# Two head groups of attention in one burst: four bursts for eight in the hidden stage of tiles 5 and 6

## The chip, the cores and the metric

The kernel runs on one core of a Trainium2 chip. Its time is device microseconds of that core, the median of several executions; before the change three executions took 805.23, 806.70 and 808.77 us. Five engines work side by side: TensorE (PE; its weight loads are shown apart as PEld), VectorE (DVE), ScalarE (ACT), GpSimd (POOL) and SyncE (SP). In this kernel POOL and SP mostly issue DMA transfers. Each engine works off its own list of instructions, whose order is fixed when the program is built.

## The reference

Attention within chunks of 64 tokens, for 8 batches of 8 heads (576 tokens, head width 64), and then a feed-forward layer with a quadratic activation over all 4608 tokens (512 wide, hidden width 2048), all in fp32:

```
scores = scale * matmul(q_c, k_c^T)            # per head and chunk: 64 x 64
attn   = exp(scores - max) / (sum + 1e-9)
x      = matmul(attn, v_c)                     # back to (4608, 512)
h      = x @ w_in                              # 2048 wide
g      = where(h >= 1, h, where(h <= -1, 0, (h + 1)^2 / 4))
out    = g @ w_out
```

## The kernel before

The 4608 tokens are nine tiles of 512. A tile's attention is four head groups (two heads each); a group's work has a number, its turn, from 0 to 35 (`turn`, L174). For tiles 3 and later, a pair of tiles shares eight turns: tiles 7 and 8 have the turns 28 to 35.

The feed-forward layer of tiles 3 to 8 is done for pairs of tiles (3 and 4, 5 and 6, 7 and 8), by a Strassen scheme with seven products where plain blocks have eight, named P1 to P7. A pair has two stages. The hidden stage (h) has 56 products of `product` (L908), each six matmuls of 128x512: eight blocks p by seven names, ordered by `alternating` (L863), in the banks ps_h0, ps_h1 for even p and ps_o0, ps_o1 for odd p. ACT and DVE read each product's bank (`whole_last`, L1008) before the next product may write it. The output stage has 56 products of `products` (L1113), by name: P1, P2, P6, P5, P7, P3, P4, eight each. Each needs its block split into a high and a low half, by an ACT cast and a DVE subtraction (`operand_of`, L1100; they run in the helpers at L743 and L747). The banks ps_o2 and ps_o3 (the pair `o_pair`) take P1, P6, P7 and P4 of the output stage of tiles 3 and 4, and nothing in a hidden stage.

Attention of the next pair is put among the products in bursts (`burst`, L1289). A burst is the values of turn n (`values_of`, L487: attention by v) and the scores of turn n + 2 (`scores_of`, L465: q by k), both in the bank pair `a_pair` (ps_a), in matmuls of 64x64. Behind it stand the softmax of the scores (`attn_softmax`, L525: a maximum on DVE, eight exponentials on ACT at L547, sum, reciprocal, multiplication and transposition on DVE, then eight DMAs into aT, four from SP's queue and four from POOL's), a copy of the values to SBUF (`keep_x`, L766), the DVE transpositions of q and k of turn m + 1 into qT and kT (`attn_turn`, L449), and loads of v, q and k. `BURSTS` (L965) holds the numbers of the products ahead of which a burst is listed: eight in the stages of tiles 3 and 4 and eight in the hidden stage of tiles 5 and 6 (every seventh product from the fourth on). Tiles 7 and 8 have none.

The order on each engine is not the order of the listing. `Plan` (L19) takes every step with an engine, a cost in us and what it reads and writes, and emits the steps in the order in which they would start by these costs; where several are ready, the one listed first goes first (`ahead` moves a step up or down in that). So a burst that is listed later can be emitted sooner, where PE would have nothing else by these costs.

Of the kernel before, what the change touches and what calls it, by code (L numbers as in the profile page):

```python
# [134 lines left out]
def kernel(  # L135
# [23 lines left out]
    NP = H // 2  # L159
# [10 lines left out]

    BATCH = (0, 1, None, 2, 3, 4, 5, 6, 7)
    ALONE = 2

    def turn(t, g):  # L174
        if t <= ALONE:
# [82 lines left out]
    def room(name, bufs, t, g):  # L258
        if t == 0 and (name, g) in first:
            return first[name, g]  # L260
        if t > 0 and name in ("e", "x"):
            return wheel[(2 * turn(t, g) + (name == "x")) % 3]
        return bufs[turn(t, g) % len(bufs)]
# [223 lines left out]
    def values_of(t, g):  # L487


        akey, aT = room("aT", aT_bufs, t, g)  # L490
        vkey, v_sb = room("v", v_bufs, t, g)
        pkeys, pair = bank_pair_of(t, g)
        halves = aT.rearrange("p (e c q) -> p c e q", e=2, q=Q)

        def emit():
            for n in range(CT // 2):
                for h in range(2):
                    at = (2 * n + h) * C
                    of = h * HALF + n * C
                    for half in range(2):  # L500
                        rows = slice(half * C, (half + 1) * C)
                        nc.tensor.matmul(  # L502
                            out=pair[h * C:(h + 1) * C, half, HALF + n * C:HALF + (n + 1) * C],
                            lhsT=v_sb[rows, of:of + C],
                            rhs=aT[rows, at:at + C] if t == 0 else halves[rows, of // C],
                            start=True, stop=True,
                        )

        return emit, (f"{akey}_0", f"{akey}_1", vkey), pkeys

    def attn_products(*some, lag=0.0):

        plan.add(
            "pe", 0.2 + 0.6 * len(some), lambda: [emit() for emit, _, _ in some],
            [k for _, reads, _ in some for k in reads],
            [k for _, _, writes in some for k in writes],
            columns=1024 * len(some), lag=lag,
        )

    def bank_pair_of(t, g):  # L520
        if t == 0 and g % 2:
            return ("ps_o2", "ps_o3"), o_pair
        return ("ps_a0", "ps_a1"), a_pair

    def attn_softmax(t, g):  # L525
# [14 lines left out]
        if sums:  # L540
            plan.add("dve", 0.08, lambda: nc.vector.tensor_scalar_mul(mx, mx, -SCALE), (), (mkey,))  # L541

            many = 2 if t > ALONE else 1

            def exps(some):
                for n in range(some * G // many, (some + 1) * G // many):
                    nc.scalar.activation(  # L547
                        out=e3[:, n, :], in_=sc[:, n // 4, n % 4, :], func=AF.Exp, bias=mx[:, n, :],
                        scale=SCALE, accum_out=sm[:, n, :],
                    )  # L550

            for some in range(many):
                plan.add("act", 2.33 / many, lambda some=some: exps(some), (*pkeys, mkey), (ekey, skey))
        else:
            plan.add("dve", 0.6, lambda: nc.vector.tensor_tensor(
                out=e4, in0=sc, in1=mx4.broadcast_to([P, 2, G // 2, C]), op=ALU.subtract
            ), (*pkeys, mkey), (ekey,))
            plan.add("act", 0.52, lambda: nc.scalar.activation(
                out=e, in_=e, func=AF.Exp, scale=SCALE
            ), (), (ekey,))  # L560
# [36 lines left out]
    def attn_split(t, g):  # L597
        if t > ALONE:
            keep_x(t, g)
            return  # L600
        pkeys, pair = bank_pair_of(t, g)
        hkey, xh = xh_bufs[g][t % 2]
        lkey, xl = xl_bufs[g][t % 2]

        def of_tokens(x):
            return x.rearrange("p (n r q) -> p r n q", r=2, q=C)

        ps = pair[:, :, HALF:].rearrange("p r (n q) -> p r n q", q=C)
        plan.add("act", 0.48, lambda: nc.scalar.copy(out=of_tokens(xh), in_=ps), pkeys, (hkey,))
        plan.add("dve", 0.6, lambda: nc.vector.tensor_tensor(  # L610
            out=of_tokens(xl), in0=ps, in1=of_tokens(xh.bitcast(F32)), op=ALU.subtract
        ), (*pkeys, hkey), (lkey,))
# [152 lines left out]

    def keep_x(t, g):  # L766
        i = g // 2
        pkeys, pair = bank_pair_of(t, g)
        name = "eo"[g % 2] + "BA"[(t - ALONE) % 2]
        key, ap = raw_of(t, i, name)  # L770
        keep(key, ap, pkeys, pair[:, :, HALF:].rearrange("p r (n q) -> p r n q", q=C))
        if t <= ALONE + 2 and name == "oB":
            combine_whole(t, i)
# [188 lines left out]
        return f"h_{f}", lambda: held["h"][:, f, :]  # L962

    LATER = -60
    BURSTS = ((10, 17, 24, 38, 45, 52, 59, 68), range(3, 53, 7))  # L965
    sums = {
        (name, p): dram.tile([P, 2, QC], F32R, name=f"sums_{name}_{p}")
        for name in OUT_ORDER for p in range(NQ)
# [320 lines left out]
    def burst(n, m):  # L1289
# [12 lines left out]
        if m is not None and m + 2 < ALL:  # L1302
            load_heads(*AT[m + 2], "qk")

    for t in range(ALONE + 1):
        for j in range(NF):
            step = (t - 1) * NF + j
            if t == 0:
                for what, g in SECOND.get(j, ()):
                    what(*divmod(NP + g, NP))  # L1310
            elif step in SPREAD:
                n, m = SPREAD[step]
                if n is None and m == 2 * NP:
                    attn_turn(*AT[m])
                burst(n, m)
                if m is not None and m + 1 <= 3 * NP + 1:
                    attn_turn(*AT[m + 1])
            ffn_in(t, j)
            prepare_next()
            m = t * NF + j - LAG  # L1320
            if m >= 0:
                ffn_out(*divmod(m, NF))
            ffn_split(t, j)
            if step in WEIGHTS:
                combine_weights(WEIGHTS.index(step), step in AGAIN)
            if step in SUMS_AT:
                combine_out(SUMS_AT.index(step), step in AGAIN)
            if t == 1:
                for name in ("P4",) if j % 2 else ("P1", "P2"):
                    keep_factor(name, j // 2, f"split_{t}_{j}")  # L1330
            if t == ALONE and j < len(HANDED):
                hand_lot("wi", j, F32 if j < 2 else F32R, *HANDED[j])
                if j == 2:
                    hand_lot("wo", 0, F32R, "ring0")
        if t:
            take_raws((first_raw, next_raw)[t - 1], t % 2)
# [11 lines left out]
        take(f"ring_{key}", key, [P, T], F32R, (key,), (f"ring_{key}",))  # L1348

    def between(t, n):  # L1350
        if turns and n in BURSTS[(t - ALONE - 1) // 2]:
            burst(*turns.pop(0))

    turns = [(n, n + 2) for n in range((ALONE + 3) * NP, ALL - 2)] + [(ALL - 2, None), (ALL - 1, None)]
    for t in range(ALONE + 1, NTILE, 2):
        if t > ALONE + 1:
            move_blocks()
        for n, (p, name) in enumerate(alternating(0, NQ)):
            between(t, n)
            if t == ALONE + 1 and name == "P1":  # L1360
# [72 lines left out]
```

## Time and profile before

| what | before |
|---|---|
| median of three executions | 806.70 us |
| the profiled execution, whole | 805.89 us |
| its span on the core | 804.1 us |
| PE busy | 795.0 us (99% of the span) |
| DVE, ACT busy | 650.2 us (81%), 537.7 us (67%) |
| granted TensorE clock, mean | 0.999 of full speed |
| hidden stage of tiles 5 and 6 | from 486.0 us to about 568 us |

The profile shows one execution. Matmuls are pipelined: a matmul's own duration overlaps with the next, so the time from one start to the next start tells what it costs. An engine's idle time stands in brackets with what ended it. The chain of waits follows the work that ended last, back from the end, so a step that isn't on it can become longer or shorter, to some extent, with no effect.

### The profile page before, as it was taken

The numbers are of one execution on the slowest core, as the hardware profiler recorded it, in microseconds if no ns is written. First come the engines' busy times: TensorE is split into PE (matmuls) and PEld (weight loads), VectorE is DVE, ScalarE is ACT, GpSimd is POOL, SyncE is SP. The second block draws the span as 40 slices with busy tenths as digits, with TensorE's granted clock in tenths as the row PEclk, the third lists the DMA queues.
The fourth block names the chain that finished last, engine by engine and source line by source line (L and its number), as shares of the span: only waits on it lengthen the run. The fifth ranks groups of instructions, "written<-read, shape, count | busy, mean of one in ns | idle before, by whom it ended". The sixth has DMA issues, their size and how long they took to land.

```text
span 804.1 us, 16928 instructions
## 1 busy us (share of the span) xinstructions
PE 795.0 (99%) x5652; PEld 652.8 (81%) x5652; DVE 650.2 (81%) x1131; ACT 537.7 (67%) x1293; POOL 345.5 (43%) x606
## 2 busy tenths in 40 slices
PE   8999999999999999999999999999999999999997
PEld 8887788888888888888888788888888888888886
DVE  5999996768799996686899996777996955589962
ACT  5799975455576775687894665887845556686450
POOL 2122223565655464554455334545343334433340
PEclk9999999999999999999999999999999999999999
DMA  9899843887998897999999899977686896666775
GB/s 223 249 302 239 221 78 127 252 261 228 293 255 225 199 283 207 302 264 250 259 246 273 217 245 256 257 230 214 184 214 197 223 243 195 194 191 195 218 200 118
DMA packets 289495, 181.51 MB, mean 226 GB/s; under 512 B 242945, under 2 KB 254721, under 8 KB 289409
## 3 DMA queue, kind: packets, MB, share of 16 engines
q0 software_dynamic: 40640, 122.72, 48.0%
q1 hardware_dynamic: 244544, 56.93, 33.7%
q10 hardware_dynamic: 4224, 0.79, 0.6%
q8 instruction: 45, 0.74, 0.4%
q14 instruction: 42, 0.34, 0.1%
HBM read 133.17 MB, written 38.80 MB: 214 GB/s over the span
## 4 chain that ended last, share of the span: by engine, by line
PE 84%; DMA 5%; DVE 4%; SPq 3%; ACT 2%; issue 2%; POOL 1%; DVEq 0%; POOLq 0%; ACTq 0%
PE ps_o L1124 17%; PE ps_o L661 15%; PE ps_h L625 15%; PE ps_h L918 13%; PE ps_o L918 13%; PE ps_h L1124 7%; PE ps_a L502 2%; SPq L382 2%; DVE new_wi L747 2%; PE ps_a L480 2%; DMA v_sb<-in_v_dram 1%; DMA k_sb<-in_k_dram 1%; DMA words<-in_moe_w_in_dram 1%; DMA q_sb<-in_q_dram 1%; DMA ring_r<-sums_P 1%
## 5 line engine op out<-in xcount | busy, mean ns | idle before, releaser
L747 DVE TENSOR_TENSOR new_wi<-new_wi,new_wi 128x512 fp32r<-128x512 f32 (+2 forms) x191 | 121.4, 668 | 13.7 <-ACT new_wi L743 12.0
L743 ACT CAST new_wi<-new_wi 128x512 fp32r<-128x512 f32 x157 | 94.3, 626 | 56.8 <-DVE new_wi L747 28.9
L625 PE MATMUL ps_h<-xh,parts 128*128 128x512 f32 x384 | 129.8, 398 | 0.0
L661 PE MATMUL ps_o<-parts,gh 128*128 128x512 f32 x384 | 118.2, 389 | 0.0
L580 POOL DMA_DIRECT2D aT<-e x96 | 50.6, 534 | 80.4 <-DVE r L636 46.0
L625 PEld LDWEIGHTS ps_h<-xh,parts 128*128 128x128 f32 x384 | 72.0, 188 | 16.0
L661 PEld LDWEIGHTS ps_o<-parts,gh 128*128 128x128 f32 x384 | 72.1, 188 | 15.0
L661 PE MATMUL ps_o<-parts,gl 128*128 128x512 f32 x192 | 74.7, 389 | 0.0
L949 DVE SCALAR_TENSOR_TENSOR new_wi<-h,new_wi 128x512 f32<-128x512 f32 x63 | 42.3, 683 | 26.1 <-ACT new_wi L948 26.1
L547 ACT ACTIVATE e<-ps_a,mx 128x64 f32<-128x64 f32 x168 | 50.8, 327 | 11.3 <-DVE mx L541 8.2
L948 ACT ACTIVATE new_wi<-new_wi 128x512 f32<-128x512 f32 x84 | 51.2, 627 | 1.2
L625 PE MATMUL ps_h<-x_parts,parts 128*128 128x512 f32 x128 | 50.1, 391 | 0.9 <-DVE x_parts L610 0.9
L945 ACT ACTIVATE new_wi<-h 128x512 f32<-128x512 f32 x63 | 39.4, 632 | 17.0 <-DVE h L939 17.0
L644 ACT CAST gh<-r 128x512 fp32r<-128x512 f32 x48 | 29.8, 620 | 30.0 <-DVE r L636 18.9
L661 PEld LDWEIGHTS ps_o<-parts,gl 128*128 128x128 f32 x192 | 36.0, 188 | 7.5
L747 DVE TENSOR_TENSOR new_wi<-new_wi 128x512 f32<-128x512 f32 (+2 forms) x64 | 39.4, 629 | 0.5
L636 DVE SCALAR_TENSOR_TENSOR r<-ps_h,r 128x512 f32<-128x512 f32 x48 | 32.6, 680 | 8.8 <-ACT r L635 8.6
L646 DVE TENSOR_TENSOR gl<-r,gh 128x512 fp32r<-128x512 f32 x48 | 32.7, 683 | 8.0 <-ACT gh L644 5.8
L1124 PE MATMUL ps_o<-new_wi,new_wo 128*128 128x512 f32 x156 | 37.6, 390 | 0.0
L580 POOL DMA_DIRECT2D aT<-x x48 | 24.7, 519 | 29.6 <-issue 13.8
L632 ACT ACTIVATE r<-ps_h 128x512 f32<-128x512 f32 x48 | 29.0, 604 | 11.8 <-PE ps_h L625 11.8
L547 ACT ACTIVATION_READ_ACCUMULATOR e<-ps_a,mx 128x1 f32 x168 | 36.7, 218 | 0.0
(232 smaller groups left out, 2074.9 us busy)
## 6 DMA issues: line engine op xcount, KB each, us to landing
ring_r<-combos POOLq DMA_DIRECT2D x36, 256.0 KB, 3.6
new_wo<-sums_P POOLq DMA_DIRECT2D x36, 256.0 KB, 3.2
new_wi<-combos POOLq DMA_DIRECT2D x34, 256.0 KB, 4.2
new_wi<-sums_P POOLq DMA_DIRECT2D x34, 256.0 KB, 3.5
ring_gh<-combos POOLq DMA_DIRECT2D x33, 256.0 KB, 3.7
ring_gl<-combos POOLq DMA_DIRECT2D x33, 256.0 KB, 3.8
ring_gh<-sums_P POOLq DMA_DIRECT2D x33, 256.0 KB, 3.9
ring_gl<-sums_P POOLq DMA_DIRECT2D x33, 256.0 KB, 3.4
```

Source lines behind the costliest of these rows:

```text
L547: nc.scalar.activation(out=e3[:, n, :], in_=sc[:, n // 4, n % 4, :], func=AF.Exp, bias=mx[:, n, :], scale=SCALE, accum_out=sm[:, n, :],)
L580: queues[queue].dma_start(out=aT[b:b + Q, to], in_=x[a:a + Q, of])
L625: nc.tensor.matmul(out=ps, lhsT=weight["wi", j][:, half, kc * P:(kc + 1) * P], rhs=x, start=(kc == 0 and i == 0), stop=(kc == KC - 1 and i ...
L646: plan.add("dve", 0.6, lambda: nc.vector.tensor_tensor(out=gl, in0=now(r), in1=gh.bitcast(F32), op=ALU.subtract), (rkey, ghkey), (glkey,), ...
L661: nc.tensor.matmul(out=acc, lhsT=x[:, cols], rhs=weight["wo", j][:, half, :], start=(j == 0 and i == 0), stop=(j == NF - 1 and i == 2),)
L743: "act", cost, lambda: nc.scalar.copy(out=out(), in_=src()), reads, writes, ahead=ahead
L747: plan.add("dve", cost, lambda: nc.vector.tensor_tensor(out=out(), in0=one(), in1=two(), op=op), reads, writes, port=True, ahead=ahead)
L918: nc.tensor.matmul(out=ps, lhsT=w()[:, at:at + P], rhs=y(), start=name in FRESH and i == 0 and k == 0, stop=i == 1 and k == 2, skip_group_ ...
L945: plan.add("act", 0.52, lambda: nc.scalar.activation(out=now(r), in_=h(), func=AF.Relu, bias=0.5, scale=0.5), (hkey,), (rkey,), ahead=50)
L948: plan.add("act", 0.52, lambda: nc.scalar.square(out=now(r), in_=now(r)), (), (rkey,), ahead=50)
L949: plan.add("dve", 0.6, lambda: nc.vector.scalar_tensor_tensor(out=now(r), in0=h(), scalar=1.0, in1=now(r), op0=ALU.max, op1=ALU.min), (hke ...
L1124: nc.tensor.matmul(out=acc, lhsT=w[:, half, b], rhs=x(), start=name in alone and p == 0 and k == 0, stop=p == NQ - 1 and k == 2, skip_grou ...
```

## The change

The eight bursts of the turns 28 to 35 become four, each with the values of two turns and the scores of two turns, by the new function `two_bursts`. The list `BURSTS` of that stage is now (3, 20, 37, 51). The second turn's values and scores go to the banks ps_o2 and ps_o3 (`beside`), and q and k of every second turn from 30 on are transposed into two of the `tmp` buffers, since qT and kT hold the first turn's. The eight exponentials of a turn are listed in four steps of two, not in two steps of four. The transpositions of turn 31 are listed ahead of the hidden stage.

```
-        pkeys, pair = bank_pair_of(t, g)
+        pkeys, pair = bank_pair_of(t, g, "values")
...
+        if name in ("qT", "kT") and turn(t, g) >= TWOS and turn(t, g) % 2:
+            return tmp_bufs[name == "kT"]
...
-            "pe", 0.2 + 0.6 * len(some), lambda: [emit() for emit, _, _ in some],
+            "pe", 0.2 + 0.6 * len(some) if len(some) < 3 else 0.57 + 0.46 * len(some), lambda: [emit() for emit, _, _ in some],
...
+    beside = set()
+
+    def bank_pair_of(t, g, what="scores"):
+        if (t == 0 and g % 2) or (what, turn(t, g)) in beside:
             return ("ps_o2", "ps_o3"), o_pair
         return ("ps_a0", "ps_a1"), a_pair
...
-            many = 2 if t > ALONE else 1
+            many = 4 if turn(t, g) >= TWOS else 2 if t > ALONE else 1
...
-    BURSTS = ((10, 17, 24, 38, 45, 52, 59, 68), range(3, 53, 7))
+    BURSTS = ((10, 17, 24, 38, 45, 52, 59, 68), (3, 20, 37, 51))
...
+    def two_bursts(ns):
+        ms = [n + 2 for n in ns if n + 2 < ALL]
+        beside.update((("values", ns[1]), ("scores", ns[1] + 2)))
+        attn_products(
+            *(values_of(*AT[n]) for n in ns), *(scores_of(*AT[m]) for m in ms), lag=0.8
+        )
+        for m in ms:
+            attn_softmax(*AT[m])
+        for n in ns:
+            attn_split(*AT[n])
+        for m in ms:
+            if m + 2 < ALL:
+                load_heads(*AT[m + 2], "qk")
+        for n in ns:
+            if n + 2 < ALL:
+                load_heads(*AT[n + 2], "v")
+        for m in ms:
+            if m + 2 < ALL:
+                attn_turn(*AT[m + 2])
...
+        if t == ALONE + 3:
+            attn_turn(*AT[TWOS + 1])
```

The change moves instructions. On PE, in the output stage of tiles 3 and 4 before the change (the rows ps_o_135 are the pair ps_o2, ps_o3, here P6; ps_o_137 and ps_o_138 are ps_o0 and ps_o1, here P5):

```order
L1124 MATMUL ps_o_135<-new_wi_3_2691,ring_gh_3706 128x512 x6
L1124 MATMUL ps_o_135<-new_wi_7_3029,ring_gl_3707 128x512 x6
L502 MATMUL ps_a<-aT_78,v_sb_72 64x64 x16
L480 MATMUL ps_a<-kT_75,qT_74 64x64 x16
L1124 MATMUL ps_o_135<-new_wi_5_2885,ring_gh_3735 128x512 x6
L1124 MATMUL ps_o_135<-new_wi_9_3176,ring_gl_3736 128x512 x6
L1124 MATMUL ps_o_137<-new_wi_6_2961,new_wo_2_2724 128x512 x3
L1124 MATMUL ps_o_138<-new_wi_6_2961,new_wo_2_2724 128x512 x3
```

and the same place with the change:

```order
L1129 MATMUL ps_o_135<-new_wi_3_2691,ring_gh_3706 128x512 x6
L1129 MATMUL ps_o_135<-new_wi_7_3029,ring_gl_3707 128x512 x6
L1129 MATMUL ps_o_135<-new_wi_5_2885,ring_gh_3735 128x512 x6
L1129 MATMUL ps_o_135<-new_wi_9_3176,ring_gl_3736 128x512 x6
L1129 MATMUL ps_o_137<-new_wi_6_2961,new_wo_2_2724 128x512 x3
L1129 MATMUL ps_o_138<-new_wi_6_2961,new_wo_2_2724 128x512 x3
```

The burst of the values of turn 28, which is listed for the hidden stage, stood between the sixth and the seventh product of P6 here; now nothing stands between them. On PE, at the start of the hidden stage of tiles 5 and 6 with the change (ps_h_139 and ps_h_140 are ps_h0 and ps_h1):

```order
L923 MATMUL ps_h_139<-new_wi_4_2808,ring_r_3683 128x512 x3
L923 MATMUL ps_h_139<-new_wi_7_3029,ring_r_3683 128x512 x3
L505 MATMUL ps_a<-aT_78,v_sb_72 64x64 x16
L505 MATMUL ps_o_135<-aT_79,v_sb_73 64x64 x16
L483 MATMUL ps_a<-kT_75,qT_74 64x64 x16
L483 MATMUL ps_o_135<-tmp_133 64x64 x16
L923 MATMUL ps_h_140<-new_wi_4_2808,ring_r_3695 128x512 x3
L923 MATMUL ps_h_140<-new_wi_8_3115,ring_r_3695 128x512 x3
```

The first burst of the new kind stands behind the third product of the stage. The next stand 17 and 15 products later and, with values alone, 17 products after that. Behind the first of them ACT's list now reads (with the change; `snaps` and `h` are copies for the products' own sums, L950 and L953 their activations):

```order
L748 COPY raw_2437<-ps_a 128x2x4x64
L748 COPY raw_2438<-ps_o_135 128x2x4x64
L552 ACTIVATE e_76,sm_83<-ps_a,mx_81 128x64 x2
L748 COPY snaps<-ps_o_137 128x512
L552 ACTIVATE e_76,sm_83<-ps_a,mx_81 128x64 x2
L552 ACTIVATE x_80,sm_84<-ps_o_135,mx_82 128x64 x2
L748 COPY h<-ps_h_139 128x512
L552 ACTIVATE e_76,sm_83<-ps_a,mx_81 128x64 x2
L552 ACTIVATE x_80,sm_84<-ps_o_135,mx_82 128x64 x2
L552 ACTIVATE e_76,sm_83<-ps_a,mx_81 128x64 x2
L950 ACTIVATE new_wi_13_3480<-h 128x512
L950 ACTIVATE new_wi_14_3584<-h 128x512
```

The exponentials of two turns alternate with the copies and activations of the products, where before those of one turn stood in two groups of four.

## Rows read from the trace of the kernel before

**Rows 1.** The page's first part: busy time, share of the span, instructions.
```profile
PE 795.0 (99%) x5652; PEld 652.8 (81%) x5652; DVE 650.2 (81%) x1131; ACT 537.7 (67%) x1293; POOL 345.5 (43%) x606
```
**Rows 2.** By stretch: length; PE, PEld, DVE, ACT, POOL busy; clock; DMA, GB/s.
```profile
410.00:486.00 76.00, 75.83 (x493) 62.05 (x484) 75.22 (x133) 47.20 (x121) 34.07 (x65) 1.00 0.95 246
...
499.60:567.70 68.10, 68.10 (x649) 55.43 (x649) 53.27 (x97) 56.93 (x161) 33.64 (x64) 1.00 0.84 228
...
644.00:722.00 78.00, 78.00 (x346) 64.54 (x345) 46.42 (x72) 51.62 (x93) 30.65 (x58) 1.00 0.70 207
...
800.00:804.00 4.00, 0.00 (x0) 0.00 (x0) 0.00 (x0) 0.00 (x0) 0.00 (x0) 0.80 0.58 96
```
**Rows 3.** PE in order of time (start, duration), output stage of tiles 3 and 4.
```profile
437.97 0.69 PE L502 MATMUL ps_a<-aT,v_sb 64*64 64x64 f32 x32
...
439.06 1.66 PE L1124 MATMUL ps_o<-new_wi,ring_gh 128*128 128x512 f32 x6
...
441.92 2.98 PE L1124 MATMUL ps_o<-new_wi,new_wo 128*128 128x512 f32 x12
444.74 0.61 PE L1124 MATMUL ps_o<-new_wi,new_wi 128*128 128x512 f32 x2
445.52 1.65 PE L1124 MATMUL ps_o<-new_wi,new_wi 128*128 128x512 f32 x6 [0.17 <-DVE new_wi L747]
```
**Rows 4.** The chain of waits in order of time: start, length, what.
```profile
438.27 7.21 DVE new_wi L747 x12
445.52 40.64 PE ps_o L1124 x178
...
502.44 1.36 PE ps_h L918 x6
```
**Rows 5.** DVE in order of time, the same place.
```profile
441.17 0.68 DVE L747 TENSOR_TENSOR new_wi<-new_wi,new_wi 128x512 fp32r<-128x512 f32 x1
...
444.79 0.68 DVE L747 TENSOR_TENSOR new_wi<-new_wi,new_wi 128x512 fp32r<-128x512 f32 x1
```
**Rows 6.** PE in order of time, hidden stage of tiles 5 and 6.
```profile
498.24 1.52 PE L918 MATMUL ps_o<-new_wi,new_wo 128*128 128x512 f32 x6
499.69 0.69 PE L502 MATMUL ps_a<-aT,v_sb 64*64 64x64 f32 x32
...
500.78 1.66 PE L918 MATMUL ps_o<-new_wi,new_wi 128*128 128x512 f32 x6
502.27 0.84 PE L918 MATMUL ps_h<-low,new_wi 128*128 128x512 f32 x3
...
521.37 0.69 PE L502 MATMUL ps_a<-aT,v_sb 64*64 64x64 f32 x32
...
551.07 2.88 PE L918 MATMUL ps_o<-new_wi,ring_r 128*128 128x512 f32 x12
553.89 0.69 PE L502 MATMUL ps_a<-aT,v_sb 64*64 64x64 f32 x32
554.51 1.66 PE L918 MATMUL ps_h<-new_wi,ring_gl 128*128 128x512 f32 x6
556.01 0.84 PE L918 MATMUL ps_o<-low,ring_gh 128*128 128x512 f32 x3
```
**Rows 7.** PE in order of time, first tile: two values bursts side by side.
```profile
26.99 0.69 PE L502 MATMUL ps_o<-aT,v_sb 64*64 64x64 f32 x32
27.50 0.66 PE L502 MATMUL ps_a<-first,first 64*64 64x64 f32 x32
```
**Rows 8.** ACT in order of time: from first exponential to the copy behind them.
```profile
503.15 0.31 ACT L547 ACTIVATE x<-ps_a,mx 128x64 f32<-128x64 f32 x1 [0.37 <-DVE mx L541]
...
505.96 0.64 ACT L743 COPY h<-ps_o 128x512 f32<-128x512 f32 x1
```
**Rows 9.** DVE in order of time: the transposition that ends this softmax.
```profile
508.48 0.71 DVE L588 STREAM_TRANSPOSE e<-x 128x512 f32<-128x512 f32 x1
```
**Rows 10.** SP's queue in order of time: the DMAs into aT.
```profile
509.25 3.17 SPq L580 DMA_DIRECT2D aT<-e x4
```
**Rows 11.** DMA issues (KB each, us to landing), at 509 to 513 and 552 to 556.
```profile
aT<-e SPq DMA_DIRECT2D x4, 32.0 KB, 5.2
...
aT<-x POOLq DMA_DIRECT2D x4, 32.0 KB, 3.1
```

More of the change, by code (lines that the diff above doesn't have):

```diff
@@ L172 @@
     ALONE = 2
+    TWOS = (ALONE + 5) * NP + 2
     def turn(t, g):
@@ L518, in attn_products @@
         )
-    def bank_pair_of(t, g):
-        if t == 0 and g % 2:
+    beside = set()
+    def bank_pair_of(t, g, what="scores"):
+        if (t == 0 and g % 2) or (what, turn(t, g)) in beside:
             return ("ps_o2", "ps_o3"), o_pair
@@ L600, in attn_split @@
             return
-        pkeys, pair = bank_pair_of(t, g)
+        pkeys, pair = bank_pair_of(t, g, "values")
         hkey, xh = xh_bufs[g][t % 2]
@@ L767, in keep_x @@
         i = g // 2
-        pkeys, pair = bank_pair_of(t, g)
+        pkeys, pair = bank_pair_of(t, g, "values")
         name = "eo"[g % 2] + "BA"[(t - ALONE) % 2]
@@ L1350, in between @@
     def between(t, n):
-        if turns and n in BURSTS[(t - ALONE - 1) // 2]:
+        if not turns or n not in BURSTS[(t - ALONE - 1) // 2]:
+            return
+        if t == ALONE + 1:
             burst(*turns.pop(0))
+        else:
+            two_bursts([turns.pop(0)[0] for _ in range(2)])
     turns = [(n, n + 2) for n in range((ALONE + 3) * NP, ALL - 2)] + [(ALL - 2, None), (ALL - 1, None)]
```

## The prediction

> **What bounds the kernel now.** I read the page's busy times first: PE is busy for 795.0 of 804.1 us [rows 1], so only PE time that goes, or comes, can move the end. A busy PE can still be one that waits for nobody or one that is paced by another engine, so the stretches come next. In the output stage of tiles 3 and 4 DVE is busy for 75.22 of 76.00 us, nearly as full as PE (75.83); in the hidden stage of tiles 5 and 6 PE fills 68.10 of 68.10 us while DVE and ACT have 53.27 and 56.93; in that of tiles 7 and 8, which has no bursts, 78.00 of 78.00 with 46.42 and 51.62 [rows 2]. So the products need no burst to cover a wait in a hidden stage; but in the output stage two engines are the bound side by side. The chain of waits settles which: it runs through twelve DVE steps from 438.27 to 445.52, then through PE for 40.64 us without another engine, and goes on through PE's products [rows 4]. The order shows that one of the eight bursts stands exactly in the DVE part of that chain, at 437.97 [rows 3].
>
> **What a burst costs on PE.** A product takes 1.36 us [rows 4]. From 498.24 to 502.27 there are two products and one full burst (values and scores): 4.03 - 2 x 1.36 = 1.31 us. From 551.07 to 556.01 there are three products and a burst of values alone: 4.94 - 3 x 1.36 = 0.86 us [rows 6]. A half burst followed by another of its kind takes 27.50 - 26.99 = 0.51 us [rows 7]. So 1.31 - 2 x 0.51 = 0.29 us of a full burst, and 0.86 - 0.51 = 0.35 us of a values burst, are for going from products to the small matmuls and back. A double burst pays that once: 0.29 + 4 x 0.51 = 2.33 us, the last one 0.35 + 2 x 0.51 = 1.37 us. In all: before 6 x 1.31 + 2 x 0.86 = 9.58, with the change 3 x 2.33 + 1.37 = 8.36 us. On paper 1.2 us are gained.
>
> **What is lost in the output stage.** The burst at 437.97 goes from there into the hidden stage. PE comes to its next products 1.31 us earlier, but these wait for their low halves from DVE. Before, the third matmul of the third P5 product starts at 445.52, after a wait of 0.17 us [rows 3], when the subtraction that began at 444.79 and took 0.68 us is done [rows 5]. DVE's list is the same up to there: the first DVE step of the burst that leaves, its maximum, stands behind all conversions for P5, and in the 7.21 us of the chain DVE has no gap [rows 4]. So the subtraction ends at 445.47 as before, and PE's wait grows from 0.17 to about 1.5 us, spread over the last P6 and first P5 products (the subtraction for the first of these ends at 441.17 + 0.68 = 441.85, and its product, which began at 441.92, would now begin at 440.61 [rows 3, 5]). The gain there lies between 0 and 1.31 us (all of it if DVE were ahead); I take 0, since the chain names DVE. After 445.52 PE runs 178 matmuls without a wait [rows 4], so the hidden stage starts when it did. That DVE and ACT are rid of a softmax in these 40 us is worth nothing there, since PE is late, not they.
>
> **What the hidden stage then holds.** Before: five full bursts and two of values, 5 x 1.31 + 2 x 0.86 = 8.27 us. Now 8.36 us: 0.09 us more. The first double burst stands behind three products; its banks ps_o2 and ps_o3 are free once two DVE transpositions behind the last P4 product have read them, two steps of 0.71 us by their kind [rows 9]; three products are 4.1 us, so I cost that wait at nothing, and it costs what DVE comes to them more than 2.7 us late. The transpositions into the `tmp` buffers and the loads are moved, not added.
>
> **The added wait: aT for the second turn.** Every value matmul waits for aT, and PE works in order, so all products queue behind it. Before, the burst at 499.69 has its softmax transposed from 508.48 on [rows 6, 9], SP issues the DMAs from 509.25 for 3.17 us [rows 10], the last of four at about 511.6, and with 5.2 us to landing [rows 11] aT is there at 516.8: 17.1 us after the burst began. It is used at 521.37 [rows 6], 21.7 us after. The second turn comes behind the first: at most one more set of exponentials (505.96 - 503.15 = 2.8 us [rows 8]), two DVE steps of 0.71 [rows 9], another 3.17 us of SP's queue, and 0.5 us because two values halves go ahead of the scores: 17.1 + 7.9 = 25.0 us. By the shorter landing, 3.1 us [rows 11], 22.9. Between the first and second double burst lie 2.33 + 17 x 1.36 = 25.5 us, and as many to the last; between the second and third 2.33 + 15 x 1.36 = 22.7, and the second turn's values come 0.6 us into the burst: 23.3. So one wait, between 0 and 1.7 us, at the third. The exponentials of the two turns alternate, which brings it nearer to the short end; I take 0.3 us.
>
> **Sum.** 0 + 0.09 + 0.3 = 0.4 us slower than the profiled execution's 805.89, so 806.3; the median shown is 806.7, 0.8 above that execution, and so I forecast 807.1 us as a median. The other ends: -1.31 in the output stage gives 805.5, the 1.7 us wait 808.5.
>
> **Rivals.**
> *The merging's gain arrives.* If DVE's list moves up by a microsecond before 445 because PE frees something earlier, the 1.2 us stay: 806.7 - 1.2 = 805.5. For it: the cost of a burst's edges is plain in rows 6. Against it: the DVE part of the chain has no gap. 0.14.
> *ACT and DVE cannot follow a double burst* (the other side). Against the stage without bursts, five softmaxes and seven copies add to ACT 56.93 - (68.10 - 8.27) x 51.62 / 78.00 = 17.3 us, to DVE 53.27 - 59.83 x 46.42 / 78.00 = 17.7 us [rows 2], some 3.5 us a burst on each. The seven products behind a double burst last 2.33 + 9.52 = 11.85 us and need 6.3 us of ACT and 5.7 of DVE themselves; with 7.0 more that is 13.3 and 12.7 us. Up to 1.4 us are over. Mostly they can slip to the next seven products, which have no burst. But the reader of a product's bank stands in the same list as the exponentials, and the next product of that bank waits for it: if nothing slips, 3 x 1.4 = 4.2 us, 811.3. It decides once a product behind a double burst waits for ACT or DVE by more than a few tenths. Against it: the list puts the copies h and snaps between the exponentials, and over the whole stage before ACT is idle for a sixth and DVE for a fifth [rows 2]. 0.10. [...]
> *The clock falls.* The granted clock is 1.00 in every stretch with matmuls and 0.80 only in the last 4 us, in which PE does nothing [rows 2]; no row tells what a denser burst does. [...] 0.02.
>
> **How the numbers follow.** The forecast's own range is 806.3 to 808.5, chance 0.70; the gain 0.14 (805.5); the overfull lists 0.10 (811.3, or 809 if half slips); the clock 0.02; the rest, 0.04, is a stall that I don't see, some 2 to 4 us slower. The three executions before lie 3.5 us apart, so a median of the changed kernel may be a microsecond or two off by itself. The range that holds 8 in 10 is 804.9 to 809.7. A measurement of this kernel can tell 0.5%, 4 us, from no change: below 802.7 there is no case, and I leave 0.02; above 810.7 lie half of the overfull lists, the clock and part of the rest, 0.08; within, 0.90.
>
> **What would show it.** In the profile of the changed kernel: no burst near 438; PE waits for DVE (new_wi, L752) between 436 and 446 of 1 to 1.7 us in all, and the hidden stage starting at 486.0 within 0.3 us; double bursts of 2.33 us from the last product's end to the regular start of the next but one; no PE idle time in the hidden stage but some tenths at the third burst. Wrong would be: a hidden stage that starts a microsecond earlier (the gain arrives), waits of ACT or DVE behind each double burst, or a clock below 1.00 there.

## The result, and the profile after

The changed kernel takes 811.0 us as a median of 16 runs (807.64 to 813.29), the kernel before 806.41 (805.23 to 808.77, 16 runs): a ratio of 1.0054, 95% interval 1.0043 to 1.0065. It is 4.6 us slower. 807.1 us was predicted, and 809.7 was the end of the range, so the median lies 1.3 us outside it.

The changed kernel's executions lie further apart than those of before, and the profiled one was the shortest of the 16 (807.64 us, span 805.6). In it the output stage takes as long as predicted. PE in order of time (start, duration), output stage of tiles 3 and 4, to be held against [rows 3]:

```profile
437.65 0.61 PE L1129 MATMUL ps_o<-new_wi,ring_gh 128*128 128x512 f32 x2
438.66 1.21 PE L1129 MATMUL ps_o<-new_wi,ring_gh 128*128 128x512 f32 x4 [0.40 <-DVE new_wi L752]
...
443.48 1.20 PE L1129 MATMUL ps_o<-new_wi,new_wo 128*128 128x512 f32 x4 [0.15 <-DVE new_wi L752]
...
445.28 0.96 PE L1129 MATMUL ps_o<-new_wi,new_wi 128*128 128x512 f32 x3 [0.15 <-DVE new_wi L752]
```

No burst stands there, PE waits for DVE three times, and the hidden stage begins at 485.76. Before, it began at 486.00, in an execution that was already 0.23 us later when the output stage began. By stretch (length; PE, PEld, DVE, ACT, POOL busy; clock; DMA, GB/s), to be held against [rows 2]:

```profile
410.00:486.00 76.00, 75.30 (x415) 60.91 (x405) 73.40 (x127) 44.69 (x103) 34.08 (x65) 1.00 0.95 243
499.60:567.70 68.10, 67.72 (x588) 55.02 (x587) 52.35 (x94) 55.29 (x156) 36.03 (x69) 1.00 0.84 232
644.00:722.00 78.00, 78.00 (x346) 64.58 (x345) 45.71 (x71) 50.78 (x90) 30.63 (x57) 1.00 0.71 208
```

PE is no longer busy throughout the hidden stage. From its first product to the first of the output stage behind it, it takes 569.32 - 485.76 = 83.56 us, before 567.74 - 486.00 = 81.74. From there to the end of the last product both take 231.4 us. So even this execution loses 1.8 us, all in the hidden stage, and the chain of waits, of which PE held 84% before, now says (shares by engine, then by line):

```profile
PE 76%; DMA 7%; DVE 6%; ACT 5%; issue 3%; POOL 1%; SPq 1%; DVEq 0%; POOLq 0%; ACTq 0%
PE ps_o L1129 17%; PE ps_h L630 15%; PE ps_o L666 15%; PE ps_h L923 10%; PE ps_o L923 9%; PE ps_h L1129 7%; DMA aT<-e 2%; DMA words<-in_moe_w_in_dram 2%; DVE new_wi L752 2%; PE ps_a L505 2%; PE ps_a L483 1%; ACT e L552 1%; DMA v_sb<-in_v_dram 1%; POOL aT L585 1%; DMA ring_r<-sums_P 1%
```

It passes through a softmax and its aT DMA. SP's queue behind the first double burst (489.93 to 492.00) says why. Before, SP was done with the loads ahead of a softmax at 508.9, before DVE had transposed it (508.48 + 0.71 [rows 9]), and issued its aT at once [rows 10]. SP's queue before:

```profile
503.76 1.93 SPq L382 DMA_DIRECT2D q_sb<-in_q_dram  x4
506.11 2.81 SPq L382 DMA_DIRECT2D k_sb<-in_k_dram  x4
```

and with the change, the last line DVE's:

```profile
486.71 5.83 SPq L1163 DMA_DIRECT2D out_dram<-new_wi  x8
492.63 3.57 SPq L401 DMA_DIRECT2D v_sb<-in_v_dram  x4
496.29 3.40 SPq L385 DMA_DIRECT2D q_sb<-in_q_dram  x4
499.79 3.50 SPq L385 DMA_DIRECT2D k_sb<-in_k_dram  x4
503.70 0.54 SPq L385 DMA_DIRECT2D q_sb<-in_q_dram  x1
504.36 3.15 SPq L585 DMA_DIRECT2D aT<-e  x4
507.55 1.11 SPq L385 DMA_DIRECT2D q_sb<-in_q_dram  x2
508.77 3.92 SPq L585 DMA_DIRECT2D aT<-e  x4
...
500.33 0.71 DVE L593 STREAM_TRANSPOSE e<-e 128x512 f32<-128x512 f32 x1
```

The first softmax was transposed at 501.04 (500.33 + 0.71), but SP first issues the loads of two head groups, and comes to its aT 3.3 us later. The wait that this makes at the second double burst is 0.22 us here. What the other executions lose is not in this profile; the runs had to find it.

### The profile page after: what moved, and what is told of

It is laid out like the page before. It is cut to its first block, busy times and chain, and to the rows that moved or that the text cites. A ratio compares the mean times of both kernels' runs of the same rounds, so it can differ in the third digit from the quotient of the medians.

```text
span 805.6 us, 16936 instructions
## 1 busy us (share of the span) xinstructions
PE 795.9 (99%) x5652; PEld 653.1 (81%) x5652; DVE 649.8 (81%) x1131; ACT 536.3 (67%) x1293; POOL 346.2 (43%) x606
## 4 chain that ended last, share of the span: by engine, by line
PE 76%; DMA 7%; DVE 6%; ACT 5%; issue 3%; POOL 1%; SPq 1%; DVEq 0%; POOLq 0%; ACTq 0%
PE ps_o L1129 17%; PE ps_h L630 15%; PE ps_o L666 15%; PE ps_h L923 10%; PE ps_o L923 9%; PE ps_h L1129 7%; DMA aT<-e 2%; DMA words<-in_moe_w_in_dram 2%; DVE new_wi L752 2%; PE ps_a L505 2%; PE ps_a L483 1%; ACT e L552 1%; DMA v_sb<-in_v_dram 1%; POOL aT L585 1%; DMA ring_r<-sums_P 1%
## 5 line engine op out<-in xcount | busy, mean ns | idle before, releaser
L552 ACT ACTIVATE e<-ps_a,mx 128x64 f32<-128x64 f32 x152 | 46.1, 331 | 10.8 <-DVE mx L546 5.3
L953 ACT ACTIVATE new_wi<-new_wi 128x512 f32<-128x512 f32 x84 | 51.7, 635 | 1.1
L950 ACT ACTIVATE new_wi<-h 128x512 f32<-128x512 f32 x63 | 39.7, 640 | 16.5 <-DVE h L944 16.4
L1129 PE MATMUL ps_o<-new_wi,ring_gh 128*128 128x512 f32 x138 | 35.3, 390 | 0.4 <-DVE new_wi L752 0.4
```

Source lines behind the costliest of these rows:

```text
L552: nc.scalar.activation(out=e3[:, n, :], in_=sc[:, n // 4, n % 4, :], func=AF.Exp, bias=mx[:, n, :], scale=SCALE, accum_out=sm[:, n, :],)
L950: plan.add("act", 0.52, lambda: nc.scalar.activation(out=now(r), in_=h(), func=AF.Relu, bias=0.5, scale=0.5), (hkey,), (rkey,), ahead=50)
L953: plan.add("act", 0.52, lambda: nc.scalar.square(out=now(r), in_=now(r)), (), (rkey,), ahead=50)
L1129: nc.tensor.matmul(out=acc, lhsT=w[:, half, b], rhs=x(), start=name in alone and p == 0 and k == 0, stop=p == NQ - 1 and k == 2, skip_grou ...
```

## The experiments

Each is an edit of the changed kernel unless it says otherwise. "Hidden stage" is the length as above, in the profiled execution. Each ratio is to runs of the kernel before that were made beside it.

| run | median us (lowest to highest, n) | ratio to before, 95% | hidden stage us |
|---|---|---|---|
| before, first profile | 806.41 (805.23 to 808.77, 16) | 1 | 81.74 |
| changed kernel | 811.0 (807.64 to 813.29, 16) | 1.0054 (1.0043 to 1.0065) | 83.56 |
| e1_again | 814.17 (813.26 to 817.67, 6) | 1.0101 (1.0084 to 1.0118) | 88.93 |
| e2_no_aT | 812.77 (807.9 to 815.91, 7) | 1.0074 (1.0049 to 1.01) | 82.72 |
| e3_spaced | 816.43 (813.21 to 819.78, 6) | 1.0123 (1.0102 to 1.0144) | 92.39 |
| e4_many2 | 812.59 (809.08 to 815.41, 6) | 1.0073 (1.0051 to 1.0095) | 87.59 |
| e8_before_shift40 | 813.66 (812.72 to 815.15, 6) | 1.0076 (1.0059 to 1.0092) | 81.74 |
| e5_shift40 | 816.45 (815.01 to 817.44, 5) | 1.0107 (1.0088 to 1.0125) | 85.70 |
| e6_shift108 | 825.47 (824.39 to 826.13, 4) | 1.0221 (1.0201 to 1.0241) | 85.70 |
| e7_shift40_no_aT | 815.24 (814.47 to 816.05, 5) | 1.0098 (1.0078 to 1.0117) | 82.58 |
| e9_again20 | 808.95 (807.41 to 816.36, 12) | 1.0046 (1.0021 to 1.0071) | 83.06 |
| e10_again20_no_aT | 808.93 (808.07 to 813.28, 12) | 1.0034 (1.002 to 1.0048) | 82.66 |
| e11_no_qk | 809.59 (808.49 to 812.31, 12) | 1.0033 (1.0022 to 1.0044) | 83.20 |
| e12_again54 | 811.1 (809.24 to 814.84, 8) | 1.0056 (1.0038 to 1.0074) | 85.94 |
| e13_again20_no_qk | 807.48 (806.31 to 808.32, 11) | 1.0009 (0.9999 to 1.0018) | 83.15 |

The changed kernel and e1_again are the same program, and their ratios, 1.0054 and 1.0101, lie further apart than their intervals. So two edits of it that were run at different times can't be told apart by some 0.5%: what follows rests on the profiles and on runs made beside each other (e1 to e4; e5 to e8; e9 to e12; e13 to e16).

**First round: waits for aT (theory A), full ACT and DVE lists (rival B), or the clock (rival C)?** e1_again is the changed kernel as it is. e2_no_aT:

```
-        halves = aT.rearrange("p (e c q) -> p c e q", e=2, q=Q)
+        halves = (v_sb if turn(t, g) >= TWOS else aT).rearrange("p (e c q) -> p c e q", e=2, q=Q)
```

> The changed kernel, unchanged, for a profile of another execution; the profiled one was the fastest of 16 (807.64 against a median of 811.0 us) and shows only 1.8 of the 4.4 us. Theory A (aT of the burst before lands late, and PE, in order, waits for it at the double bursts): a slower execution shows PE waits at L505 put down to the DMA into aT, 3 to 5 us in all at the second to fourth double burst, where the fast one shows some 0.8 us. Rival B (ACT and DVE overfull behind a double burst): the waits stand in front of products behind the bursts, released by ACT or DVE. Rival C (the clock): the granted clock in the hidden stage is below 1.00 with no waits to match. Median 811 by all three.

> Leaves out part of the computation: the values products of the last six head groups (double bursts 2 to 4) read v in place of aT, so PE waits for no aT there; the DMAs into aT still run, and the order of all instructions is the same. Theory A: the whole extra time goes, 806.4 + 0.4 = 806.8 us, 806 to 807.8. Rival B: unchanged, 811 (810 to 812), since softmax and copies are all still there. Rival C: 809 to 811, depending on whether the waits or the denser bursts lower the clock.

e3_spaced and e4_many2:

```
-    BURSTS = (..., (3, 20, 37, 51))
+    BURSTS = (..., (0, 18, 36, 52))
...
-            many = 4 if turn(t, g) >= TWOS else 2 if t > ALONE else 1
+            many = 2 if t > ALONE else 1
```

> One table changed: the double bursts come ahead of products 0, 18, 36, 52 of the stage in place of 3, 20, 37, 51, which puts two products more between the second and the third and as many as before elsewhere. Theory A: the wait at the third burst shrinks by up to 2.7 us, those at the second and fourth stay: 808 to 810 us. Rival B: as many readers behind each burst, 811. Rival C: 811.

> The exponentials of the last six head groups stand in ACT's list in two steps of four as before the change, not in four steps of two. Theory A: the transposed softmax is ready at about the same time, so 810 to 812 us. Rival B: readers of product banks are held behind 1.4 us of exponentials in place of 0.7, so 811.5 to 814 us, with waits of ACT in front of products behind the bursts.

Each theory missed. With the waits for aT taken out, the median is still 812.77 (e2_no_aT; 814.17 in e1_again beside it), so theory A alone falls. Its four executions above 812 us have a granted clock of 0.996 or 0.997, its three below 810 of 0.999 or 1.0; the profiled one is of the three. e1_again's profile shows a long execution. PE in order of time, second double burst:

```profile
516.02 0.69 PE L505 MATMUL ps_a<-aT,v_sb 64*64 64x64 f32 x32
...
517.55 0.26 PE L483 MATMUL ps_a<-kT,qT 64*64 64x64 f32 x3
517.60 0.28 PE L483 MATMUL ps_o<-tmp 64*64 64x64 f32 x3
520.75 1.12 PE L483 MATMUL ps_o<-tmp 64*64 64x64 f32 x28 [2.87 <-issue]
521.80 1.65 PE L923 MATMUL ps_o<-low,new_wi 128*128 128x512 f32 x3
523.25 1.48 PE L923 MATMUL ps_o<-new_wi,new_wi 128*128 128x512 f32 x3
```

In the middle of the fourth half, 100 matmuls into the burst, PE stops for 2.87 us with all operands there ("issue": nothing in the profile was waited for), and the three matmuls behind take 1.45 us from start to start (521.80 to 523.25), twice the 0.68 they take in the short execution (488.48 - 487.80). By stretch, the same execution:

```profile
519.00:520.00 1.00, 0.00 (x0) 0.00 (x0) 1.00 (x2) 0.24 (x1) 0.00 (x0) 1.00 1.08 326
520.00:521.00 1.00, 0.25 (x8) 0.25 (x12) 0.09 (x1) 0.00 (x0) 0.00 (x0) 0.54 1.21 270
521.00:522.00 1.00, 1.00 (x29) 0.88 (x26) 0.00 (x0) 0.08 (x1) 0.00 (x0) 0.50 0.92 170
...
526.00:527.00 1.00, 1.00 (x4) 0.78 (x3) 1.00 (x4) 1.00 (x6) 0.00 (x0) 0.55 0.51 188
527.00:528.00 1.00, 1.00 (x6) 0.82 (x5) 1.00 (x3) 0.82 (x5) 0.54 (x1) 1.00 0.20 74
```

The granted clock is 0.50 in place of 1.00 for some 6.8 us (0.92 + 5 + 0.9), in 6.2 of which PE works; at twice the time for its matmuls that costs 3.1, an estimate. Stop and clock make 6.0 us; this hidden stage is 5.4 us longer than that of the short execution, which waits for aT instead.

What was late stands in the queue that the page names q8 instruction. The page of e1_again, third part (queue: packets, MB, share of the 16 engines' span), and the same for 518.30 to 518.40 alone:

```profile
q8 instruction: 45, 0.74, 0.4%
...
q8 instruction: 1, 0.02, 66.6%
```

These are 45 packets of 16 KB (0.74 MB); PE executes 5652 matmuls and as many weight loads [rows 1], 251 for each packet. So a packet is taken for a block of PE's instructions, of 128 matmuls with their weight loads, as far as the two stops of the second round lie apart. Where one block ends and the next begins is called a border here. A double burst is 128 matmuls with their weight loads (4 x 32), as long as a block, so one border always falls into it. e1_again's packet of that place ran at 518.3, and PE goes on 2.4 us later. By the count of matmuls (128 a block) PE had crossed the border before this one at 509.6, so the packet ran 8.7 us behind it; at the borders on either side it took 2.1 and 1.5. In the short execution it ran 3.5 us behind (509.1, 512.6), in the profile before 2.2 (508.2, 510.4). There six packets in a row run 0.5 to 3.0 us behind the borders by this count (463.3, 463.8; 492.3, 495.3; 508.2, 510.4; 521.6, 522.4; 532.7, 534.7; 543.9, 545.2). Theory D, below, is the author's reading of these times: one packet runs behind each border, and at the next border PE goes on only behind it, so that it would hold the next block but one. In the kernel before, whose bursts are half a block, the profile has no wait of PE in this stage; here PE stops for 2.87 us.

e4_many2 stopped at the same matmul (1.79 us, after 0.80 for aT), and e3_spaced, whose burst begins 12 matmuls earlier in the stream, at the next one, 113 into the burst (0.63 us, after 1.89 and 1.79 for aT). In both PE goes on 2.3 to 2.8 us behind the packet (518.2 and 521.0; 521.1 and 523.5), as in e1_again. Exponentials in two steps are no worse than in four, against rival B.

**Second round: the border moved (theory D: PE stops for a late block of its instructions).** The added matmuls count as two each in the profile (x4 for the two of a line, x2 for the one, in e8_before_shift40). e5_shift40, and e6_shift108 with 6 for 2 and 9 for 10:

```
+        if n < 10:
+            nc.tensor.matmul(out=ps[:, :P // 2], lhsT=ident, rhs=ident[:, :P // 2], start=True, stop=True)
+            for _ in range(2):
+                nc.tensor.matmul(out=ps[:C, :C], lhsT=ident[:C, :C], rhs=ident[:C, :C], start=True, stop=True)
-        if n < 28 or n >= 52:
+        elif n < 28 or n >= 52:
```

> The changed kernel with 20 tiny warm-up matmuls (40 PE records, each with its weight load: 80 instructions) added in the first microseconds, so that the borders of PE's instruction blocks fall 40 records earlier in the program; nothing else is changed. Theory D (instruction fetch): PE reads its instructions in blocks of 16 KB, the next but one is fetched when a border is crossed, and a double burst is as long as a block; at the second double burst the border lies 100 records into the burst, only some 8 us behind the border before, and a fetch that takes longer in busy DMA queues stops PE there, after which the clock is halved for some us. Moved to 60 records it lies some 15 us behind it: no stall, clock 0.999 or 1.0 in every execution, 807 to 808.5 us. Theory A (PE waits for aT) and rival B (ACT and DVE overfull): the stream's place makes no difference, 811 to 814.

> The same with 54 tiny matmuls (108 records): the border lies 120 records into the second double burst, some 4 us behind the border before. Theory D: a stall in nearly every execution, 8 records before the end of that burst, 3 to 8 us with the halved clock behind it: 814 to 819 us. Theories A and B: 811 to 814 as the changed kernel, plus at most 1 us for the added warm-up.

e7_shift40_no_aT has the edit of e2_no_aT too; e8_before_shift40 is the first edit alone in the kernel before.

> Both: the 40 records, and the values products of the last six head groups read v in place of aT (part of the computation left out), so that PE waits for no aT. Theory D with aT as a smaller second cause: 806.5 to 807.5, some 0.5 us under e5_shift40. Theory D alone: as e5_shift40. Theories A and B: 806.8 and 811.

> The kernel before the change with the same 40 records, as a control: what the added warm-up costs by itself. All theories: 806.4 us within 0.7, since a single burst is half a block and leaves every fetch over 10 us.

The control missed: the warm-up costs 6.5 us by itself. So e5 and e7 are read against e8's 813.66: 2.8 and 1.6 us more, in place of 4.6 and above; e6 has no control, and its time says nothing. The profiles do. In e5_shift40 there is no stop, the clock is 0.999 or 1.0 in every execution, and the hidden stage has one wait, of 2.40 us for aT. In e6_shift108 the stop has moved, 120 matmuls into the burst as expected; PE in order of time:

```profile
533.45 0.56 PE L483 MATMUL ps_o<-tmp 64*64 64x64 f32 x23
534.92 0.29 PE L483 MATMUL ps_o<-tmp 64*64 64x64 f32 x4 [0.90 <-issue]
```

The count of matmuls from the start to the stop (by stretch; of e1_again first, then of e6_shift108) is 4208 and 4336, apart by 128, exactly a block:

```profile
0.00:520.00 520.00, 512.26 (x4208) 419.16 (x4208) 439.99 (x786) 363.42 (x940) 233.41 (x396) 1.00 0.90 239
```
```profile
0.00:534.50 534.50, 529.46 (x4336) 434.65 (x4336) 438.64 (x786) 362.81 (x940) 233.69 (x396) 1.00 0.87 232
```

The packet ran at 532.3, 2.6 us before PE goes on. That shows the stop to belong to a place in the instruction stream, not to an operand.

The control says one thing more. In e8_before_shift40, a kernel with single bursts, the packet of this place ran 8.1 us behind the border (508.4, 516.5), nearly as late as in e1_again, and PE did not stop: its next border came 14.3 us behind the last (522.7), in e1_again 8.3 us (the stop begins at 517.9). So a block that late is not new; the change brings the next border nearer.

**Third round: the border moved at no cost, and the common root (theory E: full DMA queues make both aT and the block late).** e9_again20 does 20 value matmuls (40 in the profile's count) twice, the first time where PE waits for DVE at 438; e12_again54 does so with 54:

```
+            again(*AT[TWOS - 2], 20)
             attn_turn(*AT[TWOS + 1])
...
+        plan.add("pe", 0.6, emit, (f"{akey}_0", f"{akey}_1", vkey), ("ps_a0", "ps_a1"), columns=640)
```

e10_again20_no_aT adds e2_no_aT's edit. e11_no_qk, in the changed kernel's own order:

```
-                        lambda m=m, dst=dst, src=src: load_blocks(
+                        lambda m=m, dst=dst, src=src: turn(t, g) >= TWOS + 2 or load_blocks(
```

> The changed kernel with 20 small matmuls (40 PE records) more, put where PE waits for DVE in the output stage of tiles 3 and 4: a part of the next value products, done once beforehand into the same place. The order is otherwise the same, so the borders of PE's instruction blocks fall 40 records earlier in the hidden stage, as in e5_shift40, without its dear warm-up. Theory D (a late instruction block stops PE in the second double burst, and the clock halves): no stall at L483 and no halved clock in the hidden stage; 807.5 to 809.5 us, with aT waits of up to 2.4 us left as in e5_shift40. Theory A alone (aT waits): as the changed kernel, 811 to 814.

> The same 40 records, and the values products of the last six head groups read v in place of aT (part of the computation left out). Theories D and A together, as two causes: both are gone, 806.7 to 807.7 us, the level of the kernel before plus 0.5. If 809 or more: a third cause is open.

> The changed kernel in its own order with the loads of q and k for the last four head groups left out (old heads are used; part of the computation left out). Theory E, the common root: the DMA queues are full between 490 and 520 (share 1.0 to 1.1), and the instruction block and aT are late because of the loads in them. Then the block comes within 3 us of the border at 510, aT within 4 us of its issue, and the time is 806.5 to 808 us. If the block or aT are late for another reason: 811 to 814.

> As e9_again20 with 54 small matmuls (108 records): the border lies 120 records into the second double burst, 4 us behind the border before. Theory D: PE stops 8 records before that burst's end in nearly every execution, for 1 to 6 us and as much again by the halved clock: 812 to 818 us, of which 0.5 are the added matmuls. Theory A alone: 811.5 to 814.5, with no stall of that kind.

e9_again20 falls in two: seven executions of 807.4 to 809.3 us, five of 813.2 to 816.4. e10 and e11 are by their ratios each 0.2% better than the changed kernel, about half of what was expected, and less than two sets of that kernel differ by. e12 missed low: in its profile PE waits 2.21 us for aT ahead of the border, and the late block (packet at 518.6, border at 521.0) holds it up by only 0.14. So one wait can hide the other.

e10 leaves something over. No value matmul of the last six groups waits for aT in it, its border is moved, and still its median is 808.93, where its expectation leaves a third cause open from 809 on. Three of its twelve executions took 811.68, 811.83 and 813.28 us, with a granted clock of 0.999 each. So neither the clock nor a wait of those matmuls made these long, and none of them was profiled: whether by a third cause, or by a late block at another border, is open.

**Fourth round: the loads and the border together, and a long execution of e9_again20.** e13 joins the edits of e9 and e11; e14 adds to e9:

```
+                for _ in range(2 if turn(t, g) >= TWOS else 1):
-                queues[queue].dma_start(out=aT[b:b + Q, to], in_=x[a:a + Q, of])
+                    queues[queue].dma_start(out=aT[b:b + Q, to], in_=x[a:a + Q, of])
```

> Both of e9_again20 (borders of the instruction blocks 40 records earlier) and e11_no_qk (loads of q and k for the last four head groups left out, part of the computation left out). If late blocks and late aT together, both from full DMA queues, make up all the slow executions: no execution over 810.5, median 807.5 to 808.5. If executions of 811 to 816 stay: a third cause.

> As e9_again20, with every DMA into aT of the last six head groups issued twice (3 us more in SP's queue for each, and as much in POOL's). If the slow executions of e9_again20 (813 to 816 of 807 to 816) are aT waits long enough to halve the clock: PE waits for aT by 3 to 6 us at the second and third double burst, the clock there is 0.50, and every execution takes 814 to 824 us, no instruction block late. If aT doesn't matter beyond its own wait: 810 to 813 with a clock of 1.00.

e13 is what theories A and D together ask for: eleven executions within 2.0 us, 807.48, not to be told from the kernel before. Its profile has no wait for aT and no stop. It leaves out the loads whole, though, so whatever else these do goes with them, and the changed kernel itself was not run beside it. ACT's and DVE's lists are those of the changed kernel, so these alone do not make the loss. SP's queue in e13:

```profile
492.56 4.72 SPq L401 DMA_DIRECT2D v_sb<-in_v_dram  x4
501.40 7.07 SPq L585 DMA_DIRECT2D aT<-e  x8
```

SP starts on aT at 501.40 and is done at 508.5, 4.2 us ahead of the changed kernel, and its DMAs land in 3.0 us (median) where those of e1_again take 5.7. The DMA engines' share from 500 to 520 us is 0.79, against 1.03 and 1.10 in the short execution and e1_again, and 0.99 in the kernel before. The instruction packet for the border in the second double burst (at 516.9) runs at 506.5, 10.4 us ahead. It runs 6.3 us behind the border before it (500.2), all the same, and 3.7 in e11_no_qk: it is in time by the moved border. That the loads make the block late is not shown; for aT it is.

e14 overshot: 860.76 us (859.77 to 864.89, 4 runs; ratio 1.0681, 1.0656 to 1.0706). The doubled DMAs made the rings late too (4.2 us of waits for a ring buffer, 31 for aT, 4.9 marked issue, of which 1.7 stand 64 matmuls from the nearest border). PE's pauses of 9 us have a clock of 0.50 in them and behind; as a test of aT alone it is inconclusive.

e15 to e18 are e9_again20 again, for a profile of a long execution.

> e9_again20 once more for a profile: five of its twelve executions took 813 to 816 us, but the profiled one 807.67. In a slow one: aT waits of 2.5 to 4 us at the second double burst with a halved clock behind them (theory A), no wait marked issue at L483 (theory D).

> The same, a second profile, for the chance that the first falls on a fast execution; the same expectations.

> e9_again20 once more for a profile, still for a slow execution (813 to 816 us). In it: aT waits of 2.5 to 4 us at the second double burst with a halved clock behind them (theory A); or a wait marked issue in a burst, by an instruction block over 16 us late (theory D again).

> The same kernel, a last profile, for the chance that the one before falls on a fast execution again; the same expectations.

They took 808.3, 809.26, 808.96 and 812.94 us; the kernel before beside the last two 807.83. The waits for aT at the second double burst were none, 0.8, 0.8 and 3.8 us. The last, PE in order of time:

```profile
516.07 0.69 PE L505 MATMUL ps_a<-aT,v_sb 64*64 64x64 f32 x32
520.58 1.07 PE L505 MATMUL ps_o<-aT,v_sb 64*64 64x64 f32 x29 [3.81 <-DMA aT<-e]
```

SP's queue in the same execution:

```profile
495.64 2.61 SPq L401 DMA_DIRECT2D v_sb<-in_v_dram  x4
498.33 3.77 SPq L385 DMA_DIRECT2D q_sb<-in_q_dram  x4
502.20 4.30 SPq L385 DMA_DIRECT2D k_sb<-in_k_dram  x4
506.90 0.31 SPq L385 DMA_DIRECT2D q_sb<-in_q_dram  x1
507.33 2.42 SPq L585 DMA_DIRECT2D aT<-e  x4
509.80 1.11 SPq L385 DMA_DIRECT2D q_sb<-in_q_dram  x2
512.12 3.18 SPq L585 DMA_DIRECT2D aT<-e  x4
```

And by stretch:

```profile
519.00:520.00 1.00, 0.00 (x0) 0.00 (x0) 0.53 (x1) 0.00 (x0) 0.00 (x0) 1.00 1.22 272
...
522.00:523.00 1.00, 1.00 (x48) 1.00 (x45) 0.00 (x0) 0.35 (x1) 0.00 (x0) 0.50 0.58 125
...
526.00:527.00 1.00, 1.00 (x6) 0.81 (x6) 1.00 (x4) 0.70 (x2) 0.37 (x1) 1.00 0.00 0
```

Theory A as expected: SP's stores into out_dram end at 495.5, in the short execution at 492.5, the loads follow, and SP begins on the second group's aT 3.4 us later than there (512.12, 508.77). PE waits 3.81 us, and the clock is halved for 3.4 us behind it; nothing is marked issue. Two causes, then, at the same burst: aT issued behind stores and loads on SP, and PE's instruction block. Each was followed by a half clock in one profile (e18, e1) and left the clock at full in another (e5, e6).

No version that computes the whole reference beat the kernel before. How often each cause decides an execution of the changed kernel is open: two of its executions were profiled, the shortest of 16 and e1_again's.

## Why the prediction was wrong

- **The output stage** was right: its length to the hidden stage is 79.31 us, before 79.32 (485.76 - 406.45, 486.00 - 406.68). The gain is 0, for the reason given. The waits in brackets are 0.7 us in all; from start to start, the 26 matmuls from 437.65 to 445.28 take 7.63 us, and at a sixth of 1.36 us each they would take 5.9, so PE loses 1.7 us there, the upper end of what was forecast.
- **The bursts' own cost** was near for one burst and too low for the stage: the first double burst is 2.3 us by the products on either side (488.48 to 493.50, less two products). In e10_again20_no_aT and e9_again20, whose profiles have no wait of PE in the hidden stage and a clock of 1.00, it is 0.92 and 1.32 us longer than before and not 0.09. Some 0.5 of that lies behind the third double burst, where 0.2 to 0.3 us in several profiles are a wait for DVE (h, L944): rival B in small. Some 0.5 more lie in the last three bursts of e9, each 0.17 us longer than in e10, where they read no aT; why is not shown, nor where the rest goes.
- **The added wait for aT is the step that failed**: "at most one more set of exponentials ..., two DVE steps of 0.71, another 3.17 us of SP's queue ... So one wait, between 0 and 1.7 us, at the third", and with it "The transpositions into the `tmp` buffers and the loads are moved, not added." Moved they are, on SP past the aT DMAs: two groups' q and k loads, 8.6 us of SP between 496.29 and 508.66 (3.40 + 3.50 + 0.54 + 1.11), stand ahead of the second aT, and its first DMA is issued 3.5 us behind its transposition (505.30, 508.77), 6.3 in e18 (505.84, 512.12). It was to be there 25.0 us behind the burst's start; it came after 26.5 us in the short execution (516.44 - 489.93) and 30.1 in e18 (520.58 - 490.48), against 26.1 at hand. So the wait is at the second burst and not at the third, and 0.2 to 3.8 us in place of 0.3 where it shows at all (e1_again has none). The 5.2 us for landing was about right (median 6.4 in the short execution, 5.8 in e18).
- **The instruction block was in no step.** The prediction counted a burst's matmuls as PE time and not as instructions, and so put this wait at nothing without a reason. The stop is 0.6 to 2.9 us where it shows (e1, e3, e4, e6), and in e1_again, the one long execution of the changed kernel that was profiled, it and the clock behind it make all of the loss over the short one.
- **The clock** had 0.02, because the dense bursts were thought to bring it down. They don't (1.00 through the first double burst in each profile), and no run shows a time above 810.7 by them. The clock falls to 0.50 behind some of PE's pauses, at an estimated 1.7 to 3.1 us each (half of 3.4 us in e4_many2 and e18, of 6.2 in e1_again); in e3_spaced it was at half for 10.2 us.
- **The overfull lists** had 811.3 us at 0.10, the right time for a wrong reason: e13 has these lists and 807.48.

In sum, of the 4.6 us some 0.9 to 1.3 are the bursts themselves (the stages of e10 and e9). The rest goes, as far as the profiles show, with the two waits and the clock: e13, which has neither wait, leaves 0.7 (807.48 against 806.81 beside it). How the rest divides between them, and what made e10's three long executions, stays open.

## What to carry to other kernels

Where a change moves loads, read the queue that they are moved on: here 8.6 us of loads on SP came to stand ahead of the second aT, and the wait appeared at its first consumer (the second double burst, 0.22 us in the short execution and 3.81 in e18), not at the tightest distance on paper (the third). Count a dense run of small matmuls in instructions as well as in time: here a double burst is as long as a block of the instruction stream (128 matmuls), the next border came 8.3 us behind the last in place of 14.3 (e1_again, e8), and a block as late as one that did no harm before (8.1 us in e8, 8.7 in e1_again) stopped PE for 2.87 us. And profile more than one execution when their times spread; the shortest showed 1.8 of 4.6 us. Run the unedited kernel beside each set of edits, too: here two sets of it differ by 0.5%.

## What the runs showed of the hardware

- A late instruction block stopped PE in the middle of a burst (2.87, 1.79, 0.90 and 0.63 us), at a place in the stream that is the same in three kernels (matmul 4208 or 4209) and a whole block of 128 matmuls on in a fourth. PE went on 2.3 to 2.8 us behind the block's packet.
- PE pauses of 2.40 us (e5_shift40), of 2.21 (e12), and of 1.27 and 0.90 close together (e6) left the clock at 1.00; 0.80 and 1.79 close together (e4), 2.87 (e1) and 3.81 (e18) were followed by 0.50 for 3.4 to 6.8 us, the three pauses of e3 by 10.2. By what rule is not shown.
- The added warm-up was dear (6.5 us in e8_before_shift40). Four 64x64 matmuls of it, all on the same 64 partitions in and out and in one bank, take 0.62 us from start to start (13.08 to 13.70), as long as the 32 of a burst half, whose partitions and banks go in turns (17.77 to 18.39). The 128x128 warm-up matmuls take 0.21 us each (four in 14.61 to 15.46), in the kernel before from 8.12 on 0.12 (eight in 0.99); by stretch the granted clock is 1.00 at both places (14 to 17 us, 8 to 10 us), so what makes either difference isn't shown. In e8_before_shift40:

```profile
13.08 0.69 PE L1384 MATMUL ps_h<-ident 64*64 64x64 f32 x4
...
14.61 1.06 PE L1386 MATMUL ps_h<-ident 128*128 128x128 f32 x4
...
17.77 0.69 PE L480 MATMUL ps_a<-kT,qT 64*64 64x64 f32 x32
```
